# Three small ScalarE copies of a unit's maxima, queued three slots later

## The chip, the cores and the metric

The kernel runs on one core of one Trainium2 chip. The time is the device time of one execution in microseconds (us); "before" is the median of three runs. One further execution was taken with the hardware profiler, and the views of the profile below are of that one.

Engine names: PE is TensorE's matmuls, PEld its weight loads, DVE is VectorE, ACT is ScalarE, POOL is GpSimd, SP is SyncE, which issues most DMAs.

## The reference

One token sequence `x` (2048 x 576) goes through an attention block with 32 heads of 18 columns and through a GELU MLP with 4608 hidden columns; a gate per token mixes the two. All arrays are float32.

```python
qkv = (x @ wqkv)                      # heads: 32, 18 columns each
scores = einsum("bhqd,bhkd->bhqk", q, k) * 18 ** -0.5
a = einsum("bhqk,bhkd->bhqd", softmax(scores), v) ... @ wo
b = gelu(layernorm(x) @ w1 + b1) @ w2 + b2
g = sigmoid((x * gate_w).sum(-1, keepdims=True))
return g * a + (1 - g) * b
```

## The kernel before, in words

Attention runs over 32 **units**; a unit is one pair of heads and one half (1024) of the queries. Each unit has two stages. The **first stage** (`s1_round`, 32 rounds a unit) multiplies queries by keys with the queries as output rows (L204, one matmul for each head of the pair), and VectorE takes the maximum of each 128 x 512 result (L206). When all rounds of a unit are done, `s1_finish` turns the maxima into two extra rows of the query operand: VectorE's maximum over the four key blocks, negated (L215); three ScalarE copies that round it and lay it out (L216 to L218: `nmh`, the rounded value; `nm`, its negative; `nm2`, its place in the layout); VectorE's sum of pairs, which gives the rest that rounding lost (L222); a transposition (L223); and eight small DMAs that write the rows into the query tile (`qa<-mr`, issued on line 114 by a helper).

The **second stage** (`s2`) multiplies keys by queries with those rows included (L280, 56 rows in place of 54), so that the maximum is already subtracted, and ScalarE's exponential (L282) takes the result out of PSUM into a tile `p` or `ring`. `ps_s2` has two PSUM banks, so a score matmul L280 waits for the exponential of the matmul two before it. The product with the values (L309, `pv`) follows for each pair of steps. First-stage rounds of a later unit are woven between the two heads of a second-stage step, so four score matmuls stand together in TensorE's order: L280, L204, L204, L280.

The MLP fills the rest of TensorE: L548 is the first matmul and L680 the second. Its activation runs on VectorE (L572, bias), ScalarE (L573, bias of the other half; L636, squares; L629, tanh) and POOL (L160). ScalarE also rounds weights (L445) in the first quarter.

The order of the work is written out by the program: `run_due` is called after each piece and counts one **slot**; `defer(n, fn)` queues `fn` so that it is issued n slots later. Each engine then runs its own instructions in the order in which they were issued. `looped[0]` is true once the loop over units has begun. The maxima of unit 0 are finished before that. Two of the 32 units find SP busy with loads (`aside`); their eight DMAs are issued by ScalarE, one a slot.

Of the kernel before, what the change touches and what calls it, by code (L numbers as in the profile page):

```python
# [9 lines left out]
F32 = mybir.dt.float32  # L10
F32R = mybir.dt.float32r
AF = mybir.ActivationFunctionType
# [47 lines left out]
def gated_mix_kernel(ctx: ExitStack, tc: tile.TileContext, x, wqkv, wo, w1, b1, w2, b2, gate_w, out):  # L60
    nc = tc.nc
# [50 lines left out]
    def dma_r(queue, dst, src):  # L112

        queue.dma_start(dst.bitcast(F32), src)
# [5 lines left out]
    def defer(n, fn):  # L120
        later.append((slot[0] + n, fn))
# [87 lines left out]
    def s1_finish(u):  # L209

        m4 = M4.pop(u)
        nm = asm.tile([P, 2, 2, 8], F32, name="nm")
        nm2 = asm.tile([P, 2, 2, 8], F32, name="nm2")
        nmh = asm.tile([P, 2, 8], F32R, name="nmh")
        nc.vector.tensor_reduce(nm[:, 0], m4, axis=AX.X, op=ALU.max, negate=True)  # L215
        nc.scalar.activation(nmh, nm[:, 0], AF.Copy)  # L216
        nc.scalar.activation(nm[:, 1], nmh.bitcast(F32), AF.Copy, scale=-1.0)
        nc.scalar.activation(nm2[:, :, 0, :], nmh.bitcast(F32), AF.Copy)  # L218

        def rows():  # L220
            mr = asm.tile([P, 32], F32, name="mr", bufs=1)
            nc.vector.tensor_reduce(nm2[:, :, 1, :], nm.rearrange("p k a b -> p a b k"), axis=AX.X, op=ALU.add)  # L222
            nc.vector.transpose(mr, nm2.rearrange("p a b c -> p (a b c)"))  # L223
            qa = QA[u % 3]
            aside = slot[0] < ybusy[0]

            def store(h, k):
                r = 64 * h + 54
                c = 32 * k + 16 * h
                dst = qa[r:r + 2, :].rearrange("b (t k n) -> b t k n", k=4, n=32)[:, :, k, :]  # L230
                dma_r(nc.scalar if aside else nc.sync, dst, mr[c:c + 16, :])
            for n in range(8):
                if aside:
                    defer(1 + n, lambda n=n: store(*divmod(n, 4)))
                else:
                    store(*divmod(n, 4))
        defer(2 if looped[0] else 8, rows)

    RING = []
    ybusy = [0]  # L240
# [104 lines left out]
    looped = [False]  # L345

    def take_round():
        u, r = rounds.pop()
        head = s1_round(u, r)
        if r == NR - 1:  # L350
            defer(1, lambda: s1_finish(u))
        return head
# [1029 lines left out]
```

## Time and profile before

| | before |
|---|---|
| time, median of 3 runs | 2275.35 us (2274.24 to 2276.49) |
| time of the profiled execution | 2275.04 us |
| its span, first to last instruction | 2273.2 us |
| PE busy | 2243.9 us (99%) |
| PEld busy | 1647.7 us (72%) |
| DVE busy | 1654.6 us (73%) |
| ACT busy | 1442.5 us (63%) |
| POOL busy | 946.5 us (42%) |
| mean granted clock of TensorE | 0.998 |

Busy times of different engines overlap. Matmuls are pipelined and their ends are modelled, so two matmuls that run one after the other count as busy just as two that run side by side. An engine's idle time is listed with what ended it, its releaser.

### The profile page before, as it was taken

Reading aid. Unit: us, or ns where it says so; the run is one execution under the profiler, and the core shown is the slowest. Engines: PE = TensorE matmul, PEld = TensorE weight load, DVE = VectorE, ACT = ScalarE, POOL = GpSimd, SP = SyncE. Lnnn points to the kernel's source line nnn. Section 1 sums busy time; section 2 is a strip of 40 time slices with the busy share of each in tenths; the row PEclk is TensorE's granted clock in tenths of the full one; section 3 lists DMA queues with packets and bytes.
Section 4 is the critical chain, followed back from the end, with each engine's and each line's share of the span. In section 5 each row is a group of like instructions: output and inputs, shape, how many; then the busy total and the mean of one; then the engine's idle time right before and its main releaser. Section 6 shows DMA issues by size and latency. Waiting matters only on the chain.

```text
span 2273.2 us, 51149 instructions
## 1 busy us (share of the span) xinstructions
PE 2243.9 (99%) x20569; PEld 1647.7 (72%) x20569; DVE 1654.6 (73%) x2889; ACT 1442.5 (63%) x2719; POOL 946.5 (42%) x936
## 2 busy tenths in 40 slices
PE   8999999999999999999999999999999999999999
PEld 7878767777667777677776777677767777777668
DVE  5675777777777787777777877787777777777545
ACT  4223777777776666666666666676666666666661
POOL 4002456666663434443444444434444444444420
PEclk9999999999999999999999999999999999999999
DMA  7755634536483524232363324233365233323355
GB/s 241 259 188 182 195 128 153 157 132 183 142 243 135 168 95 124 98 119 98 94 183 143 119 90 142 85 116 116 121 166 157 97 120 113 106 98 115 106 172 196
DMA packets 163219, 323.62 MB, mean 142 GB/s; under 512 B 59646, under 2 KB 86178, under 8 KB 152146
## 3 DMA queue, kind: packets, MB, share of 16 engines
q1 hardware_dynamic: 158982, 313.57, 43.6%
q10 hardware_dynamic: 4000, 6.78, 0.8%
q8 instruction: 162, 2.65, 0.5%
q14 instruction: 75, 0.61, 0.1%
HBM read 229.07 MB, written 95.16 MB: 143 GB/s over the span
## 4 chain that ended last, share of the span: by engine, by line
PE 91%; DVE 4%; DMA 3%; ACT 2%; issue 0%; SPq 0%; POOL 0%; ACTq 0%; DVEq 0%
PE ps L309 20%; PE ps L548 19%; PE ps L680 18%; PE ps L280 13%; PE ps L204 11%; PE ps L956 5%; DVE m L206 2%; PE ps L974 2%; PE ps L1264 1%; PE ps L871 1%; DMA ka<-ot_scr 0%; ACT p L282 0%; DMA dn_scr<-dn 0%; DMA x<-ot_scr 0%; PE ps L1005 0%
## 5 line engine op out<-in xcount | busy, mean ns | idle before, releaser
L206 DVE TENSOR_REDUCE m<-ps 128x1 f32<-128x512 f32 x2048 | 1302.6, 684 | 324.5 <-PE ps L204 293.2
L282 ACT ACTIVATE p<-ps 128x512 f32<-128x512 f32 x1368 | 743.1, 596 | 370.0 <-PE ps L204 275.3
L280 PE MATMUL ps<-qa,ka 56*128 56x512 f32 x2048 | 712.7, 415 | 13.4 <-ACT p L282 6.8
L204 PE MATMUL ps<-ka,qa 54*128 54x512 f32 x2048 | 650.5, 418 | 3.6 <-DVE m L206 2.4
L280 PEld LDWEIGHTS ps<-qa,ka 56*128 56x128 f32 x2048 | 359.8, 185 | 246.3 <-issue 100.1
L680 PE MATMUL ps<-w,hh 64*128 64x288 f32 x4352 | 528.0, 297 | 1.5 <-DVE x L654 0.8
L548 PE MATMUL ps<-big,w 64*128 64x512 f32 x3888 | 517.6, 392 | 0.6 <-POOL w L160 0.5
L160 POOL TENSOR_SCALAR zz<-zz 128x512 f32<-128x512 f32 x272 | 168.8, 621 | 799.6 <-ACT zz L636 793.9
L282 ACT ACTIVATE ring<-ps 128x512 f32<-128x512 f32 x680 | 369.2, 595 | 187.3 <-PE ps L204 135.8
L548 PEld LDWEIGHTS ps<-big,w 64*128 64x128 f32 x3888 | 395.1, 185 | 60.1 <-POOL w L160 0.9
L680 PEld LDWEIGHTS ps<-w,hh 64*128 64x128 f32 x4352 | 418.7, 186 | 15.8 <-PE ps L680 1.3
L160 POOL TENSOR_TENSOR zz<-zz,z 128x512 f32<-128x512 f32 x280 | 361.4, 1291 | 34.9 <-ACT zz L638 10.5
L680 PE MATMUL ps<-w,hl 64*128 64x288 f32 x2176 | 358.4, 292 | 0.0
L204 PEld LDWEIGHTS ps<-ka,qa 54*128 54x128 f32 x2048 | 336.6, 185 | 29.4 <-DVE m L206 9.4
L309 PE MATMUL ps<-p,vt 128*32 128x512 f32 x2736 | 344.5, 598 | 0.0
L680 PEld LDWEIGHTS ps<-w,hl 64*128 64x128 f32 x2176 | 244.0, 186 | 1.2
L160 POOL TENSOR_TENSOR w<-x,w 128x576 fp32r<-128x576 f32 (+1 forms) x34 | 68.3, 2011 | 289.0 <-ACT w L445 286.9
L309 PEld LDWEIGHTS ps<-p,vt 128*32 128x32 f32 x2736 | 71.4, 109 | 152.2 <-issue 146.3
L160 POOL TENSOR_TENSOR hl<-zz,hh 128x512 fp32r<-128x512 f32 x134 | 174.0, 1299 | 15.3 <-ACT hh L599 4.5
L309 PE MATMUL ps<-ring,vt 128*32 128x512 f32 x1360 | 179.1, 598 | 0.0
L654 DVE SCALAR_TENSOR_TENSOR x<-ps,x 128x288 f32<-128x288 f32 x270 | 110.9, 452 | 90.1 <-PE ps L680 87.8
L956 PE MATMUL ps<-big,wqk 128*128 128x512 f32 x504 | 123.6, 400 | 0.0
(119 smaller groups left out, 1380.4 us busy)
## 6 DMA issues: line engine op xcount, KB each, us to landing
w<-w_scr SPq DMA_DIRECT2D x54, 1152.0 KB
w<-w_scr SPq DMA_DIRECT2D x108, 576.0 KB
w_scr<-w SPq DMA_DIRECT2D x18, 1152.0 KB
w_scr<-w SPq DMA_DIRECT2D x36, 576.0 KB
qa<-qk_scr SPq DMA_DIRECT2D x192, 72.0 KB
ka<-qk_scr SPq DMA_DIRECT2D x90, 144.0 KB
x<-in_B_w_dram SPq DMA_DIRECT2D x34, 288.0 KB
qk_scr<-hh SPq DMA_DIRECT2D x36, 256.0 KB
```

The lines of the kernel that those rows point to most:

```text
L160: fn(*args, **kw)
L204: nc.tensor.matmul(ps, qa[r0:r0 + 54, t * P:(t + 1) * P], ka[r0:r0 + 54, kb * TB:(kb + 1) * TB], start=True, stop=True)
L206: nc.vector.tensor_reduce(M4[u][:, h, t, kb:kb + 1], ps, axis=AX.X, op=ALU.max)
L280: nc.tensor.matmul(ps, ka[r0:r0 + 56, kc * P:(kc + 1) * P], qa[r0:r0 + 56, qb * TB:(qb + 1) * TB], start=True, stop=True)
L282: nc.scalar.activation(RING[n % 3][:, qb, h], ps, AF.Exp, scale=SCALE)
L309: nc.tensor.matmul(OB[u][r:r + 32, :], v[:, k, 19 * h:19 * h + 32], RING[c % 3][:, qb, h, :], start=(k == 0), stop=(k == NT - 1))
L548: nc.tensor.matmul(ps[h], wt[w_][r, c, :], Y[s_][r, c, :], start=(k == 0), stop=(k == 26))
L654: nc.vector.scalar_tensor_tensor(dst, ps[nn][:, :ND], 0.5, b2b[:, cs[nn]] if base else dst, op0=ALU.mult, op1=ALU.add)
L680: mm = nc.tensor.matmul(ps[nn][:, :ND], h_[r, tok], w_[p_][r, cs[nn]], start=(k == 0 or bare and k == 3 * G), stop=(k == 6 * G - 1 or bare ...
L871: nc.tensor.transpose(ps[:, t * P:(t + 1) * P], x_view(tb)[:, t, c * P:(c + 1) * P], ident)
L956: nc.tensor.matmul(ps, w_[:, c, ms], big[:, s_, :], start=(k == 0), stop=(k == len(prods) - 1))
L974: nc.tensor.matmul(ps[:, :ND], big[:, s_, tok], w_[:, c, cs], start=(k == 0), stop=False)
```

## The change

The three ScalarE copies go into a function `parts`, issued three slots after L215 (two for unit 0) and not with it; the sum of pairs, the transposition and the DMAs (`rows`) are queued from `parts`, so two slots after the copies (eight before the loop) and not after L215.

```diff
         nc.vector.tensor_reduce(nm[:, 0], m4, axis=AX.X, op=ALU.max, negate=True)
-        nc.scalar.activation(nmh, nm[:, 0], AF.Copy)
-        nc.scalar.activation(nm[:, 1], nmh.bitcast(F32), AF.Copy, scale=-1.0)
-        nc.scalar.activation(nm2[:, :, 0, :], nmh.bitcast(F32), AF.Copy)
+
+        def parts():
+            nc.scalar.activation(nmh, nm[:, 0], AF.Copy)
+            nc.scalar.activation(nm[:, 1], nmh.bitcast(F32), AF.Copy, scale=-1.0)
+            nc.scalar.activation(nm2[:, :, 0, :], nmh.bitcast(F32), AF.Copy)
+            defer(2 if looped[0] else 8, rows)
 
         def rows():
...
-        defer(2 if looped[0] else 8, rows)
+        defer(3 if looped[0] else 2, parts)
```

Lines behind this place are three further down in the changed kernel: L282 is L285 there, L573 is L576, L636 is L639; the copies L216 to L218 become L218 to L220, and L222 and L223 become L225 and L226.

The order of instructions on ScalarE, unit 3 (424 us in the profile), before:

```order
L636 ACTIVATE zz<-z 128x512 x2
L282 ACTIVATE p<-ps 128x512 x4
L629 ACTIVATE zz<-zz 128x512
L216 ACTIVATE nmh<-nm 128x16
L217 ACTIVATE nm<-nmh 128x16
L218 ACTIVATE nm_5211<-nmh 128x2x8
L282 ACTIVATE p<-ps 128x512 x2
L629 ACTIVATE zz<-zz 128x512
L282 ACTIVATE ring_2268<-ps 128x512 x4
```

And the same place now:

```order
L639 ACTIVATE zz<-z 128x512 x2
L285 ACTIVATE p<-ps 128x512 x4
L632 ACTIVATE zz<-zz 128x512
L285 ACTIVATE p<-ps 128x512 x2
L632 ACTIVATE zz<-zz 128x512
L285 ACTIVATE ring_2268<-ps 128x512 x2
L218 ACTIVATE nmh<-nm 128x16
L219 ACTIVATE nm<-nmh 128x16
L220 ACTIVATE nm_5211<-nmh 128x2x8
L285 ACTIVATE ring_2268<-ps 128x512 x2
```

The three copies went behind two pairs of exponentials and a tanh.

ScalarE again, unit 8 (737 us), where a bias and two squares of the MLP follow, before:

```order
L216 ACTIVATE nmh<-nm 128x16
L217 ACTIVATE nm<-nmh 128x16
L218 ACTIVATE nm_9960<-nmh 128x2x8
L573 ACTIVATE z<-ps,b1t 128x512
L282 ACTIVATE p<-ps 128x512 x2
L636 ACTIVATE zz<-z 128x512 x2
L282 ACTIVATE p<-ps 128x512 x2
```

Now:

```order
L576 ACTIVATE z<-ps,b1t 128x512
L285 ACTIVATE p<-ps 128x512 x2
L639 ACTIVATE zz<-z 128x512 x2
L218 ACTIVATE nmh<-nm 128x16
L219 ACTIVATE nm<-nmh 128x16
L220 ACTIVATE nm_9960<-nmh 128x2x8
L285 ACTIVATE p<-ps 128x512 x2
```

The copies moved from ahead of the bias to right behind the squares and right ahead of a pair of exponentials.

VectorE at the end of unit 0, before the loop (239 to 247 us), before:

```order
L215 TENSOR_REDUCE nm<-m_941 128x16
L572 TENSOR_SCALAR ring_2268<-ps,b1t 128x512
L206 TENSOR_REDUCE m_2514<-ps 128x1 x2
L222 TENSOR_REDUCE nm_2456<-nm 128x2x8
L223 STREAM_TRANSPOSE mr<-nm_2456 128x32
L206 TENSOR_REDUCE m_2514<-ps 128x1 x4
```

Now:

```order
L215 TENSOR_REDUCE nm<-m_941 128x16
L575 TENSOR_SCALAR ring_2268<-ps,b1t 128x512
L206 TENSOR_REDUCE m_2514<-ps 128x1 x4
L225 TENSOR_REDUCE nm_2456<-nm 128x2x8
L226 STREAM_TRANSPOSE mr<-nm_2456 128x32
L206 TENSOR_REDUCE m_2514<-ps 128x1 x2
```

The sum of pairs and the transposition went behind one more round's pair of maxima. TensorE's and POOL's orders are the same as before.

## The prediction

> **What bounds the kernel now.** I read the page's busy times first, then the chain that ended last, then TensorE's waits, then the groups of the three instructions that move.
>
> ```profile
> span 2273.2 us, 51149 instructions
> PE 2243.9 (99%) x20569; PEld 1647.7 (72%) x20569; DVE 1654.6 (73%) x2889; ACT 1442.5 (63%) x2719; POOL 946.5 (42%) x936
> ...
> PE 91%; DVE 4%; DMA 3%; ACT 2%; issue 0%; SPq 0%; POOL 0%; ACTq 0%; DVEq 0%
> ```
>
> TensorE (PE) is busy for all but 2273.2 - 2243.9 = 29.3 us, and the chain runs over it for 91%. No other engine is near its limit, so only what TensorE waits for, or what makes its matmuls run less side by side, can be gained. Its waits, in us in total, times, longest:
>
> ```profile
> PE ps L280 <- ACT p L282: 6.8, 9, 0.8
> PE ps L280 <- ACT ring L282: 5.4, 7, 0.8
> ```
>
> These two make 16 waits and 12.2 us, by the second-stage score matmul (L280) for an exponential (L282) that must empty a PSUM bank. Who makes ScalarE late there is told by the first of the three moved instructions:
>
> ```profile
> L216 ACT ACTIVATE nmh<-nm x32: 215/216/218, 239.6 to 2137.9; 128x16 fp32r<-128x16 f32 x32
> ...
>   DVE nm L215: 31.7, 31
> ```
>
> ScalarE sits idle 31.7 us in front of L216, at 31 of its 32 places, until VectorE has made the maximum L215. One such place, in order of time (start, us, engine, line; in brackets the idle time before it and its releaser):
>
> ```profile
> 422.68 0.40 PE L280 MATMUL ps<-qa,ka 56*128 56x512 f32 x1
> 423.77 0.22 DVE L215 TENSOR_REDUCE nm<-m 128x16 f32<-128x64 f32 x1
> 424.03 0.22 ACT L216 ACTIVATE nmh<-nm 128x16 fp32r<-128x16 f32 x1 [1.21 <-DVE nm L215]
> 424.50 1.06 ACT L282 ACTIVATE p<-ps 128x512 f32<-128x512 f32 x2
> 425.13 0.49 PE L280 MATMUL ps<-qa,ka 56*128 56x512 f32 x1 [0.80 <-ACT p L282]
> 426.12 0.64 PE L309 MATMUL ps<-p,vt 128*32 128x512 f32 x4
> ```
>
> The scores of 422.68 were done at 423.08, and ScalarE was idle; but its queue is in order, and L216 stood in front of the exponential, waiting for a maximum that came at 424.00. The exponential began 1.42 us late and TensorE stood for 0.80 us. Such places go from this kind to the last and smallest one:
>
> ```profile
> 1040.81 0.49 PE L280 MATMUL ps<-qa,ka 56*128 56x512 f32 x1 [0.80 <-ACT ring L282]
> 1041.72 0.64 PE L309 MATMUL ps<-p,vt 128*32 128x512 f32 x4
> ...
> 2138.99 0.98 PE L280 MATMUL ps<-qa,ka 56*128 56x512 f32 x2 [0.55 <-ACT ring L282]
> 679.45 0.50 PE L280 MATMUL ps<-qa,ka 56*128 56x512 f32 x1 [0.40 <-ACT p L282]
> ```
>
> I count 14 of 0.80 us and one of 0.55. The sixteenth (679.45) comes 6 us after its L216 and has another cause, DMAs issued by ScalarE; it stays.
>
> **The change part by part.** Nothing is removed or added; three copies per unit go to a later place of ScalarE's queue, and L222, L223 (VectorE) and the eight DMAs (SP's queue, at two units ScalarE's) follow.
>
> *The waits themselves.* Three slots later L215 has long ended, so L216 does not wait and the exponential goes first. The 15 waits vanish: 12.2 - 0.40 = 11.8 us. What is late next at these places: the first exponential would start at about 423.1 instead of 424.50, so TensorE is held by nothing there.
>
> *What the waits do to the matmuls behind them.* After the wait the four score matmuls take 426.12 - 425.13 = 0.99 us until L309 starts, and 1041.72 - 1040.81 = 0.91 at the other. Where nothing waited:
>
> ```profile
> 301.98 0.39 PE L280 MATMUL ps<-qa,ka 56*128 56x512 f32 x1
> ...
> 302.57 0.64 PE L309 MATMUL ps<-p,vt 128*32 128x512 f32 x4
> 737.12 0.39 PE L280 MATMUL ps<-qa,ka 56*128 56x512 f32 x1
> ...
> 737.67 1.07 PE L309 MATMUL ps<-ring,vt 128*32 128x512 f32 x8
> ```
>
> That is 0.59 and 0.55 us. All of it is booked as busy, so the 29.3 us of idle time do not show it. The difference lies between 0.91 - 0.59 = 0.32 and 0.99 - 0.55 = 0.44; I take 0.33, since most of the 14 long waits look like the one at 1040.81, for 15 places: 4.9 us. The lower bound is nothing, the upper 6.6.
>
> *The copies' new place, good kind.* They take 424.50 - 424.03 = 0.47 us of ScalarE wherever they stand. At most places they now fall behind a pair of exponentials, in the idle time in which ScalarE had waited for L215 anyway (0.53 and 1.21 us at the two places shown): no cost, and the cover is that idle time. At six places (the first at 363, the last at 2077) a pair of MLP bias and squares follows, and there the copies now stand behind the squares:
>
> ```profile
> 363.22 0.22 ACT L216 ACTIVATE nmh<-nm 128x16 fp32r<-128x16 f32 x1 [0.53 <-DVE nm L215]
> ...
> 363.70 0.67 ACT L573 ACTIVATE z<-ps,b1t 128x512 f32<-128x512 f32 x1
> 366.26 1.09 ACT L282 ACTIVATE p<-ps 128x512 f32<-128x512 f32 x2
> 366.92 0.49 PE L280 MATMUL ps<-qa,ka 56*128 56x512 f32 x1
> 367.40 0.50 PE L280 MATMUL ps<-qa,ka 56*128 56x512 f32 x1
> ```
>
> The second L280 starts 0.48 after the first because it waits for the second exponential (366.26 + 1.09 = 367.35). Without the copies L573 can start up to 0.48 + 0.53 = 1.01 us earlier, if its input is there; I take 0.6, of which the copies behind the squares give back 0.47. So about 0.13 is gained there, and I put 0.07 on the pair before, whose exponentials come 0.6 earlier: 0.2 times 6 is 1.2 us (bounds: nothing, and 6 times 1.01 - 0.47, 3.2).
>
> *The copies' new place, bad kind.* At four places L573 starts only when its matmuls are done, so it gains nothing when the copies leave:
>
> ```profile
> 737.38 0.69 ACT L573 ACTIVATE z<-ps,b1t 128x512 f32<-128x512 f32 x1 [0.21 <-PE ps L548]
> 740.06 1.09 ACT L282 ACTIVATE p<-ps 128x512 f32<-128x512 f32 x2
> 741.04 0.39 PE L280 MATMUL ps<-qa,ka 56*128 56x512 f32 x1
> 741.28 0.42 PE L280 MATMUL ps<-qa,ka 56*128 56x512 f32 x1
> ```
>
> Here the exponentials move from 740.06 to 740.53; the second ends at 741.62, and the L280 of 741.28 waits for it, 0.34 to 0.39 us. The pair stretches as at 366.92, so I take 0.25 for three places: 0.75 us lost (bounds 0 and 4 times 0.39 = 1.6). The fourth (unit 15) loses a DMA issue from the same spot in exchange and is counted as nothing.
>
> *The start.* Unit 0 is finished before the loop, and its rows are waited for already:
>
> ```profile
> 243.62 0.18 DVE L222 TENSOR_REDUCE nm<-nm 128x16 f32<-128x32 f32 x1
> 243.90 0.21 DVE L223 STREAM_TRANSPOSE mr<-nm 128x32 f32<-128x32 f32 x1
> 244.04 1.29 DVE L206 TENSOR_REDUCE m<-ps 128x1 f32<-128x512 f32 x2
> ...
> 244.14 5.41 SPq L114 DMA_DIRECT2D qa<-mr  x8
> ...
> 250.65 0.79 PE L280 MATMUL ps<-qa,ka 56*128 56x512 f32 x1 [0.66 <-DMA qa<-mr]
> ```
>
> L222 now stands behind the pair of maxima that starts at 244.04 and ends at 245.33. It had followed the pair before it, of the same length, which ended at 243.70. So L223 and SP's eight DMAs start 1.63 us later, and the L280 of 250.65 too: 1.63 us lost, with nothing to hide it. Around it the clock is halved:
>
> ```profile
> 247.25:250.67 3.42, 2.30 (x19) 1.43 (x19) 2.30 (x5) 3.25 (x7) 3.05 (x3) 1.00 0.05 9
> 250.67:257.49 6.82, 6.82 (x41) 5.82 (x43) 4.42 (x7) 5.09 (x10) 3.81 (x3) 0.50 0.59 172
> ```
>
> (Window, length, busy time of PE, PEld, DVE, ACT and POOL, then the granted clock, the DMA share and GB/s.) The halved stretch follows a stretch of 3.42 us with 1.12 us idle; none of the 0.80 us waits brought one. The longer wait adds idle time here. If a further 3.41 us stretch runs at 0.50, another 1.7 us goes; if the wait merely lies inside the halved stretch, 0.8 us comes back. I take nothing for it. [...]
>
> *The rows of the other 31 units.* L222 and L223 move behind two or four more maxima, that is one or two groups of score matmuls further.
>
> ```profile
> 739.79 5.29 SPq L114 DMA_DIRECT2D qa<-mr  x8
> ...
> 751.29 0.39 PE L280 MATMUL ps<-qa,ka 56*128 56x512 f32 x1
> ```
>
> This is one of the tightest units on SP. Its last issue ends at 745.08, its first L280 comes at 751.29, and at the start the landing took 250.65 - 244.14 - 5.41 = 1.10: 5.1 us to spare. Two groups are 741.04 - 737.12 = 3.92 us, so even this unit keeps over 1 us. At some units a weight load that stood right behind the rows on SP now stands ahead of them. At the two units whose DMAs ScalarE issues, they go one pair of exponentials further. POOL's order stays as it is. Cost: nothing; the bound on the other side is rival 4.
>
> *Sum.* -11.8 - 4.9 - 1.2 + 0.75 + 1.63 = -15.5 us. The profiled execution took 2275.04 us (span 2273.2), 0.3 under the median of the three runs, so 2259.5 against 2275.04, or **2259.8 us** against 2275.35 (0.7% less). A measurement of this kernel can tell about 0.2%, 4.6 us, from no change.
>
> **The rivals.**
> 1. *Only the idle time comes back.* The stretch behind the waits belongs to that place and not to the wait. Against it: the two unstalled groups shown belong to other units and are alike. Without the 4.9 us: 2264.7.
> 2. *The halved clock lasts one stretch longer.* 2259.8 + 1.7 = 2261.5.
> 3. *The copies collide at every new place,* as at 741: 0.25 at all 31 instead of three, 7.0 us more: 2266.8. Against it stands a weight copy that takes over twice 0.47 us and stands between exponentials too, while every 0.8 us wait stands 1.1 us behind an L216:
>
> ```profile
> L445 ACT ACTIVATE w<-x 128x1152 fp32r<-128x1152 f32 x16 | 18.6, 1165 | 0.0
> ```
>
> 4. *Slower: the rows come too late.* The first L280 of each unit waits for the DMAs. It takes a shift above the 5.1 us to spare; each us beyond costs 31. At a shift of 5.6 us the 15.5 are gone; at 6.0 it is 2259.8 + 28 = 2288. It would need a third group of maxima ahead of L222, or SP held by a load.
> 5. *Nothing is gained,* because TensorE is held at the same places by a filler's input or a bank of VectorE: 2275. Against it: in the first example TensorE's next work was the four matmuls, and its maxima were done at 423.77.
>
> **How the numbers follow.** The forecast 0.62; rival 1 0.12, rival 2 0.12, rival 3 0.07, rival 4 0.04, rival 5 0.03. The first four cases are faster by more than 0.2% (0.93, of which I leave 0.01 to the unmeasured), no change is 0.04, slower 0.04. The range goes down by the upper bounds of the stretch and of the good places (1.7 + 2.0) to 2256, and up to rival 3, 2267; rivals 1 and 2 lie inside.
>
> **What would show it.** L216's new line has no idle time released by L215; TensorE's waits for L282 fall from 16 to a handful, none over 0.5 us; no four-matmul group before L309 takes 0.9; the wait for the rows at about 250 us grows from 0.66 to about 2 us and no other unit waits for them; new short waits stand only where squares precede the copies. Wrong would be: new waits at L280 for `qa<-mr`, or the 0.8 us waits moved to another pair.

## The result, and the profile after

The changed kernel takes 2261.06 us (median, 2260.56 to 2262.71), the kernel before 2275.32 us beside it (2274.24 to 2276.49, four runs). The ratio is 0.9938, with a 95% interval of 0.9921 to 0.9956. So the change gains 14.3 us; 15.5 were forecast. The profiled execution of the changed kernel took 2260.64 us.

The first lines of the profile's page of the changed kernel, and TensorE's waits in it (total us, times, longest):

```profile
span 2258.9 us, 51149 instructions
PE 2238.7 (99%) x20569; PEld 1643.0 (73%) x20569; DVE 1650.3 (73%) x2889; ACT 1441.9 (64%) x2719; POOL 946.4 (42%) x936
```

```profile
...
PE ps L283 <- DMA qa<-mr: 2.2, 2, 1.5
PE ps L204 <- DVE m L206: 2.2, 4, 0.6
PE ps L683 <- DMA w<-w_scr: 2.1, 1, 2.1
...
PE ps L283 <- ACT p L285: 0.5, 1, 0.5
```

The span is 14.3 us shorter (2273.2 to 2258.9). TensorE's idle time fell from 29.3 to 2258.9 - 2238.7 = 20.2 us, which is 9.1; the other 5.2 us are busy time that went away, on balance (2243.9 to 2238.7): matmuls run side by side again where they had queued behind a wait, as the stretch of four below shows. Of the 16 waits for the exponential (12.2 us) one is left, 0.5 us, and it is the one with another cause. But there is a wait that was not there before: 2.1 us of the second MLP matmul (L683) for a reload of its weights.

The copies no longer wait for VectorE. Of the first of them, L218, the profile says this; nothing stands under "sat idle", and one weight load (0.8 us, not a matmul) is put down to it:

```profile
L218 ACT ACTIVATE nmh<-nm x32: 200/220/237, 240.2 to 2126.5; 128x16 fp32r<-128x16 f32 x32
its engine sat idle before it (us, times) until:
who waited for it (us, times):
  PEld ps L283: 0.8, 1
```

And the place in unit 3 that the prediction showed, now (start, us, engine, line):

```profile
422.79 1.09 ACT L285 ACTIVATE p<-ps 128x512 f32<-128x512 f32 x2 [0.28 <-PE ps L283]
...
425.23 0.23 ACT L218 ACTIVATE nmh<-nm 128x16 fp32r<-128x16 f32 x1
...
423.79 0.40 PE L283 MATMUL ps<-qa,ka 56*128 56x512 f32 x1
...
424.44 1.92 PE L312 MATMUL ps<-p,vt 128*32 128x512 f32 x16
```

The exponential waits for the score matmul only, the copies follow 2.4 us behind it, TensorE stands nowhere, and the four score matmuls take 424.44 - 423.79 = 0.65 us instead of 0.99. At all fifteen places that had waited, the group of four now takes 0.34 to 0.66 us to the product with the values; it took 0.91 to 1.05.

### The profile page after: what moved, and what is told of

Same layout as the page of the kernel before. It is cut to its first block, busy times and chain, and to the rows that moved or that the text cites. A ratio compares the mean times of both kernels' runs of the same rounds, so it can differ in the third digit from the quotient of the medians.

```text
span 2258.9 us, 51149 instructions
## 1 busy us (share of the span) xinstructions
PE 2238.7 (99%) x20569; PEld 1643.0 (73%) x20569; DVE 1650.3 (73%) x2889; ACT 1441.9 (64%) x2719; POOL 946.4 (42%) x936
## 4 chain that ended last, share of the span: by engine, by line
PE 95%; DMA 2%; DVE 2%; ACT 0%; issue 0%; POOL 0%; SPq 0%; ACTq 0%; DVEq 0%
PE ps L312 21%; PE ps L551 20%; PE ps L683 20%; PE ps L283 14%; PE ps L204 11%; PE ps L959 5%; PE ps L977 2%; PE ps L1267 1%; PE ps L874 1%; DMA big<-y_scr 1%; DVE m L206 0%; DMA dn_scr<-dn 0%; DMA w<-w_scr 0%; PE ps L1008 0%; DVE x L1194 0%
## 5 line engine op out<-in xcount | busy, mean ns | idle before, releaser
L285 ACT ACTIVATE p<-ps 128x512 f32<-128x512 f32 x1368 | 743.2, 596 | 380.7 <-PE ps L204 256.0
L683 PE MATMUL ps<-w,hh 64*128 64x288 f32 x4352 | 529.6, 297 | 1.5 <-DVE x L657 0.8
L285 ACT ACTIVATE ring<-ps 128x512 f32<-128x512 f32 x680 | 369.2, 595 | 190.2 <-PE ps L204 122.1
L683 PEld LDWEIGHTS ps<-w,hh 64*128 64x128 f32 x4352 | 420.1, 186 | 16.0 <-DVE x L657 1.0
L683 PE MATMUL ps<-w,hl 64*128 64x288 f32 x2176 | 362.9, 292 | 0.0
L683 PEld LDWEIGHTS ps<-w,hl 64*128 64x128 f32 x2176 | 247.5, 186 | 1.3
```

Of the source, the lines that this page charges most:

```text
L285: nc.scalar.activation(RING[n % 3][:, qb, h], ps, AF.Exp, scale=SCALE)
L683: mm = nc.tensor.matmul(ps[nn][:, :ND], h_[r, tok], w_[p_][r, cs[nn]], start=(k == 0 or bare and k == 3 * G), stop=(k == 6 * G - 1 or bare ...
```

## The experiments

Each was compared with the kernel before on its own chip: the first four on one where that takes 2274.34 us (2273.00 to 2275.82), the other four on a second one, at 2274.15 us (2273.38 to 2275.62). Medians of different sets are compared by what each gains over its own kernel before. "Gain of a unit" below means this: in both traces I take the start of each unit's first second-stage score matmul, subtract, and look at what the difference grows by from unit to unit. The second stage of a unit holds the copies of the next one; a place is named by the unit whose copies stand in it. Unit 23 alone is named by its second stage, in which the reload falls; the stall there belongs to the copies of unit 24.

### 1. The rows later, the copies left where they were

Against the kernel before:

```diff
-        defer(2 if looped[0] else 8, rows)
+        defer(5 if looped[0] else 10, rows)
```

> The three ScalarE copies stay right behind L215 as before; only the sum of pairs, the transposition and the DMAs go three slots later (for unit 0 two), to the places that the change gave them. Theory (the wait in ScalarE's queue is all of it): the 15 waits of 0.8 us stay, TensorE waits 16 times and about 12 us for L282, the time is that of before plus the start's 0.6 to 1.6 us: 2275.3 to 2277. Rival (it is VectorE that gained, because L222 and L223 no longer stand between its additions and maxima): a good part of the 14 us is here, 2262 to 2270.

Measured: 2283.54 us (2280.69 to 2284.34), ratio 1.0038 (1.0025 to 1.0051). It is slower, and by more than either expectation. TensorE's waits:

```profile
PE ps L280 <- ACT p L282: 6.9, 9, 0.8
...
PE ps L280 <- ACT ring L282: 5.4, 7, 0.8
...
PE ps L680 <- DMA w<-w_scr: 2.1, 1, 2.1
```

The 16 waits stay as they were, so they belong to the copies alone; putting VectorE's two instructions off gains nothing. The new wait for the reload comes with the rows alone. In this profile (2280.69 us) the loss is 5.6 us of span: 2.6 at unit 23, where the reload is, 0.14 to 0.23 at eight of the fifteen stalled places, 0.5 at another and 0.7 at unit 15, the other 0.3 at the start and in small amounts. Why later rows cost 0.2 at a stalled unit is open, but it is there in the changed kernel too: those eight places gain 1.10 to 1.21 us in it, five of the others 1.24 to 1.37. The other four executions took 1.9 to 3.7 us longer than the profiled one and have mean clocks of 0.997 or 0.998 against its 0.999; more halved stretches would do that, but no trace of them was taken.

### 2. The copies later, the rows left where they were

Against the changed kernel:

```diff
-            defer(2 if looped[0] else 8, rows)
+            defer(1 if looped[0] else 8, rows)
...
-        defer(3 if looped[0] else 2, parts)
+        if looped[0]:
+            defer(1, parts)
+        else:
+            parts()
```

The order on VectorE and on SP is that of the kernel before; only ScalarE's differs.

> In the loop the copies go one slot later and the rows one slot behind them, so VectorE's and SP's orders are those of before and only ScalarE's differs; unit 0 as before. Theory: all 15 waits go, the start's loss goes too, and if the 2.1 us wait for a weight reload near 1681 us (with 3.4 us of half clock behind it) comes from TensorE being early, it stays: 2260.3; if it comes from the later rows on SP, it goes: 2256.7. Rival (the rows' later place is needed): L222 waits for the copies and VectorE's maxima hold TensorE, over 2265.

Measured: 2256.73 us (2255.11 to 2258.36), ratio 0.9924 (0.9907 to 0.9940). The wait for the reload is gone, as the theory of the late rows says: fourteen of the fifteen stalled places gain 1.18 to 1.39 us each, unit 23 among them (1.29). The median is the 2256.7 of that theory, but by luck, for it hides a new loss that was not expected: unit 7, the fifteenth, loses 1.09 us. On TensorE (the second-stage score matmul is L286 in this kernel, its exponential L288), and on ScalarE:

```profile
672.05 0.79 PE L286 MATMUL ps<-qa,ka 56*128 56x512 f32 x1 [1.75 <-ACT p L288]
```

```profile
667.12 1.06 ACT L288 ACTIVATE p<-ps 128x512 f32<-128x512 f32 x2
669.40 1.95 ACTq L114 DMA_DIRECT2D qa<-mr  x2
671.40 0.60 ACT L288 ACTIVATE p<-ps 128x512 f32<-128x512 f32 x1 [3.22 <-DMA qa<-mr]
```

Unit 7 is one of the two whose rows ScalarE sends. ScalarE was free at 668.18; the first DMA was issued only at 669.40. The semaphore that its issue waits for is raised at 669.33 by the landing of one of SP's loads (`big<-y_scr`; in the kernel before at 676.72, and the DMA is issued at 676.80), and ScalarE's order holds the exponential behind it until 671.40. In the kernel before this was the sixteenth wait, of 0.40 us.

### 3. Unit 0 back at its old place

Against the changed kernel:

```diff
-        defer(3 if looped[0] else 2, parts)
+        if looped[0]:
+            defer(3, parts)
+        else:
+            parts()
```

> The changed kernel with unit 0, before the loop, as it was. The prediction priced the start at 1.63 us: 2259.4. The trace of the changed kernel says that half of that lay inside the halved clock, net 0.6: 2260.5. The wait for the rows at about 250 us goes back from 1.5 to 0.7 us. In neither case does the wait near 1681 us change.

Measured: 2260.77 us (2257.16 to 2261.70), ratio 0.9936 (0.9921 to 0.9951). Over its own kernel before it gains 13.6 us, and the changed kernel gains 14.3 over its own; the intervals overlap almost wholly. So the whole time shows no price of the start, and settles neither the 1.63 us of the prediction nor 0.6. The trace does not settle it either: its profiled execution reaches the second stage of unit 1 by 1.8 us sooner than that of the changed kernel, but the halved clock at the start lasted 3.41 us in it and 6.83 us in the other, which is worth 1.7 us. The wait for the reload stays (2.72 us here).

### 4. The copies on GpSimd, right behind VectorE's maximum, the rows late

Against the kernel before:

```diff
-        nc.scalar.activation(nmh, nm[:, 0], AF.Copy)
...
+        one = dict(op0=ALU.mult, op1=ALU.mult)
+        nc.gpsimd.tensor_scalar(nmh, nm[:, 0], 1.0, 1.0, **one)
...
-        defer(2 if looped[0] else 8, rows)
+        defer(5 if looped[0] else 8, rows)
```

> The copies run on GpSimd right behind L215, rows at the changed kernel's places, unit 0's rows as before: ScalarE is rid of the copies altogether. Theory (what is left of their cost is the ten places where they stand next to bias and squares): L285 waits gone as in the changed kernel, and at those places the second L283 of a pair no longer waits for its exponential, up to 0.25 to 0.5 each: 2.5 to 4 us below the changed kernel with unit 0 back, 2256.5 to 2258. Rival (the new places cost nothing): equal to it, 2260.5. A third: GpSimd's activation chain is held by the wait and TensorE waits for its results, over 2262.

Measured: 2258.20 us (2255.84 to 2260.58), ratio 0.9928 (0.9913 to 0.9942). It tells the places apart. At the three places where the copies now collide with exponentials, the changed kernel loses 0.36, 0.40 and 0.38 us (units 8, 18 and 27); with the copies off ScalarE the losses are -0.04, 0.03 and 0.05. So the collision is what costs there. The reload's wait stays, as it must with late rows.

### 5. Unit 23 alone with early rows

Against the changed kernel:

```diff
-            defer(2 if looped[0] else 8, rows)
+            defer((1 if u == 23 else 2) if looped[0] else 8, rows)
...
-        defer(3 if looped[0] else 2, parts)
+        defer((1 if u == 23 else 3) if looped[0] else 2, parts)
```

> The changed kernel, but for unit 23 alone the copies go one slot behind L215 and the rows one slot later, so its transposition stands where it stood before; SP's order is the same as in the changed kernel. Theory (twelve loads of the next MLP input stand behind unit 23's rows on SP, and the rows' transposition now comes late, so all of SP's queue and at its end the weight reload come late): the 2.1 us wait near 1681 and the half clock behind it go, 3.8 us less than the changed kernel: 2257.2. Rival (TensorE simply arrives earlier at that reload): the wait stays, 2261.

Measured: 2256.99 us (2256.33 to 2257.41), ratio 0.9923 (0.9907 to 0.9940). It gains 17.2 us over its own kernel before, 2.9 more than the changed kernel, and the intervals of the two ratios overlap, so the whole time alone would not show it. The traces do: the changed kernel loses 2.72 us at unit 23, this one gains 1.09 there, so 3.81 us come back, and the wait for the reload is gone. The rival, that TensorE had merely become too early for the reload, would have left the wait: TensorE comes to it at 1679.71 here, and came at 1679.48 in the changed kernel. SyncE's queue in the kernel before, in the changed kernel and in this one, around that unit:

```profile
1649.81 5.24 SPq L114 DMA_DIRECT2D qa<-mr  x8
1655.15 10.51 SPq L114 DMA_DIRECT2D big<-y_scr  x12
...
1680.94 1.83 SPq L114 DMA_DIRECT2D w<-w_scr  x4
```

```profile
1641.22 5.55 SPq L114 DMA_DIRECT2D qa<-mr  x8
1646.87 10.22 SPq L114 DMA_DIRECT2D big<-y_scr  x12
...
1672.54 1.86 SPq L114 DMA_DIRECT2D w<-w_scr  x4
```

```profile
1638.35 5.55 SPq L114 DMA_DIRECT2D qa<-mr  x8
1644.00 10.10 SPq L114 DMA_DIRECT2D big<-y_scr  x12
...
1669.43 1.91 SPq L114 DMA_DIRECT2D w<-w_scr  x4
```

Behind the rows stand twelve large loads of the MLP's input, and behind these the weights' reload. SP issues what is behind the loads as they land, one after the other: in the changed kernel it stands 6.8 us for them before the four stores L332 alone. So the reload follows the first load by nearly the same time in all three, 25.79, 25.67 and 25.43 us, and a delay of the rows reaches it through the loads. The reader of the weights in the kernel before and in the changed one:

```profile
1692.44 0.29 PE L680 MATMUL ps<-w,w 64*128 64x288 f32 x2
```

```profile
1681.58 0.40 PE L683 MATMUL ps<-w,w 64*128 64x288 f32 x2 [2.10 <-DMA w<-w_scr]
```

By the change TensorE was there at 1681.58 - 2.10 = 1679.48, 12.96 us earlier than before; the reload was issued only 1680.94 - 1672.54 = 8.40 us earlier. Of these 4.56 us, 2.10 became a wait, so about 2.5 had been to spare. With the rows early it is issued 11.51 us earlier, and nothing waits.

### 6. Copies later, and ScalarE's own DMAs three slots later

As experiment 2, and against that

```diff
-                    defer(1 + n, lambda n=n: store(*divmod(n, 4)))
+                    defer(4 + n, lambda n=n: store(*divmod(n, 4)))
```

> The kernel in which the copies alone move (one slot), with the DMAs that ScalarE issues at units 7 and 15 three slots later, where the changed kernel has them. Theory (the first of these DMAs waits for a load on SP and holds the exponentials behind it; later, it waits less): the 1.75 us wait at 672 us falls to about 0.45, and with it the 3.4 us of half clock behind it goes: 2256.7 - 1.3 - 1.7 = 2253.7. Rival (the wait follows TensorE's pace, not the DMA's place): 2256.7.

Measured: 2251.92 us (2251.25 to 2252.83), ratio 0.9902 (0.9887 to 0.9916). Better than expected: the wait of unit 7 does not just shrink to what it was, it vanishes, since the first DMA now stands behind a pair of exponentials where its semaphore has just been raised, and the DMAs stand one at a time between exponentials:

```profile
669.12 1.09 ACT L288 ACTIVATE p<-ps 128x512 f32<-128x512 f32 x2 [0.99 <-PE ps L204]
669.74 1.24 ACTq L114 DMA_DIRECT2D qa<-mr  x1
671.03 0.60 ACT L288 ACTIVATE p<-ps 128x512 f32<-128x512 f32 x1 [0.83 <-PE ps L286]
```

Unit 7 goes from a loss of 1.09 us (experiment 2) to a gain of 2.29.

### 7. As 6, but the copies of units 8, 15, 18 and 27 stay right behind the maximum

Against experiment 6:

```diff
-            defer(1 if looped[0] else 8, rows)
+            defer((2 if u in (8, 15, 18, 27) else 1) if looped[0] else 8, rows)
...
-        if looped[0]:
+        if looped[0] and u not in (8, 15, 18, 27):
             defer(1, parts)
```

> The kernel before this one in the call, with the copies of units 8, 15, 18 and 27 alone back right behind L215, ahead of the bias. The traces say that these units lose 0.36 to 0.40 us when the copies stand behind bias or squares: 4 times 0.37 = 1.5 us less than the kernel with the later DMAs: 2252.2. If those losses come from something else that moved: equal to it.

Measured: 2251.09 us (2249.98 to 2252.27), ratio 0.9898 (0.9883 to 0.9913). At units 8, 18 and 27 the loss falls from 0.38, 0.39 and 0.49 us to 0.03, 0.03 and 0.05, 1.15 us together; 1.5 were expected with unit 15. That one gains 0.15 more, but it varies by 0.5 us between kernels that have the same order there (see below), so nothing follows from it. The medians are 0.8 apart, less than their spread, so the whole time alone would not show it.

### 8. GpSimd's copies, early rows, ScalarE's DMAs later

The three copies as in experiment 4, the rows at their slots of the kernel before, ScalarE's DMAs as in 6.

> Copies on GpSimd right behind L215, rows where they were before, ScalarE's DMAs three slots later. If GpSimd's queue is free in time: ScalarE has no copies at all, about 1.5 us less than the kernel with the later DMAs (the three to ten places with bias and squares): 2252.2. Rival: GpSimd is inside a 1.3 us operation when the maxima come, L222 waits on VectorE and TensorE's first-stage matmuls wait for banks: over 2256.

Measured: 2250.21 us (2249.08 to 2251.04), ratio 0.9894 (0.9879 to 0.9908). This is the lowest median: 23.9 us below the kernel before, and the interval lies below that of the changed kernel, 0.9921 to 0.9956. From experiment 7 it cannot be told apart, since the times of the two overlap. Next to nothing is lost at the colliding places (0.01 each), and the six places of the good kind gain 0.54 to 0.71 us instead of 0.34 to 0.45. Against the changed kernel GpSimd is busy for 20 us more and ScalarE for 12 less:

```profile
PE 2231.5 (99%) x20569; PEld 1643.4 (73%) x20569; DVE 1651.9 (73%) x2889; ACT 1429.8 (64%) x2623; POOL 966.8 (43%) x1032
```

## Why the prediction was right, and where its errors cancelled

The forecast of 2259.8 us lies 1.3 below the median, inside the range. Its main mechanism is the one that acts. But one step was wrong by about 4 us, and smaller terms made up for most of it, so that the total comes so close is partly luck. Worked out by gains of units, from the traces of before and after:

| step | forecast, us | measured, us |
|---|---|---|
| waits and the stretch behind them, 15 places | -16.7 | -16.8 at 14 places, and about -1.1 at unit 23 |
| good kind, six places | -1.2 | -2.3 |
| bad kind, three places | +0.75 | +1.1 |
| unit 15 | 0 | +0.5 |
| start | +1.63 | +0.6 |
| rows of the other 31 units | 0 | +3.8 |
| rest, and a start of the run 0.45 earlier | | -0.2 |
| sum | -15.5 | -14.4 |

*The waits, and the stretch behind them.* Right. Experiment 2 moves the copies alone and gets the gain, experiment 1 moves the rest alone and gets none. The 14 places gain 1.10 to 1.37 us each, 1.20 in the mean; the forecast was 0.80 + 0.33. That the gain is larger than the wait of 0.80, and that the four matmuls take 0.65 where they took 0.91 to 0.99, refutes rival 1: the stretch belonged to the wait, and it went at all fifteen places. Rival 5 (nothing gained) falls with it.

*The good kind.* Undersized by half. The value was picked between 0 and 3.2 us, and 2.3 came. Where the copies are off ScalarE (experiment 8) the same six places gain 3.9 us (0.54 to 0.71 each), so the copies behind the squares still take some of it.

*The bad kind, and rival 3.* The mechanism is right, as experiments 4 and 7 show. The size is not 0.25 but 0.36 to 0.40 us, about the upper bound of 0.39. In the changed kernel:

```profile
734.03 0.20 ACT L220 ACTIVATE nm<-nmh 128x16 f32<-128x16 f32 x1
734.13 1.06 ACT L285 ACTIVATE p<-ps 128x512 f32<-128x512 f32 x2
...
734.76 0.50 PE L283 MATMUL ps<-qa,ka 56*128 56x512 f32 x1
735.25 0.50 PE L283 MATMUL ps<-qa,ka 56*128 56x512 f32 x1
```

The copies push the pair of exponentials to 734.13, and the second score matmul waits for the second of them: the two stand 0.49 apart, where they were 0.24 apart in the kernel before (741.04 and 741.28). It stays at these places; at the five other places in the loop no unit lost more than 0.06, so rival 3 did not come. Unit 15, put at nothing, lost 0.52 in this trace, and why is open: it lost 0.70 in experiment 1, where its copies stay in place, and nothing in experiment 3, which has the order of the changed kernel there.

*The start.* The wait came as forecast and cost a third of it in this pair of executions. TensorE's wait there, and the stretch of halved clock around it (length, then busy time of PE, PEld, DVE, ACT and POOL, granted clock, DMA share, GB/s):

```profile
251.79 0.79 PE L283 MATMUL ps<-qa,ka 56*128 56x512 f32 x1 [1.47 <-DMA qa<-mr]
```

```profile
249.49:256.32 6.83, 5.34 (x26) 3.60 (x25) 3.96 (x7) 4.47 (x10) 3.22 (x4) 0.50 0.32 99
```

The matmul is late by 251.79 - (250.65 - 0.45) = 1.59 us, against 1.63 forecast (0.45 us is how much earlier this run was there). But of the halved stretch only 5.34 us are now busy and not 6.82, so about 0.7 us of work ran later at full clock. The prediction named this ("0.8 us comes back") and took nothing for it; it should have been taken.

In this pair the halved stretch lasts 6.83 us in both, so rival 2 (one stretch more) does not show. But it is not refuted. With early rows of unit 0 (the kernel before and experiments 2, 3, 4, 6, 7 and 8) the halved stretch at the start lasts 3.41 us in five of seven profiled executions, and 6.83 in the kernel before and in experiment 8; with late rows (the changed kernel, experiments 1 and 5) it is 6.83 in all three. The five with 3.41 reach the second stage of unit 1 by 1.2 to 1.7 us sooner than the profiled kernel before. So the 0.6 holds between two executions that both had the longer stretch, and whether late rows bring it more often is open.

*The rows of the other units: the step that failed.* The prediction checked whether the rows would reach their own reader in time, found at least 1 us to spare, and wrote "Cost: nothing". That was true of the rows: no unit but the first waits for them, so rival 4 did not come as it was written. It was not true of what is queued behind them. SP's queue is in order, and at unit 23 the late rows held twelve loads and a reload, whose reader had about 2.5 us to spare, 40 us further on. I had seen that weight loads change places with rows, and did not follow one to its reader. And the wait brought a halved stretch with it, in the changed kernel:

```profile
1676.26:1679.68 3.42, 3.22 (x32) 1.47 (x24) 2.81 (x6) 3.27 (x7) 1.58 (x2) 1.00 1.01 399
1679.68:1683.09 3.41, 1.51 (x18) 1.48 (x18) 0.96 (x3) 0.86 (x2) 2.20 (x3) 1.00 1.00 393
1683.09:1686.50 3.41, 3.41 (x28) 3.41 (x28) 1.66 (x3) 2.42 (x5) 0.00 (x0) 0.50 0.15 57
```

The wait is 2.10 us, the halved stretch costs half of 3.41, 1.7 us: 3.8. The changed kernel loses 2.72 us at this unit where it should have gained 1.1, the same 3.8. Experiment 5 gives 3.81 us back by the rows of that one unit. The DMA share of 1.01 and 1.00 in the first two rows (399 and 393 GB/s) shows the DMA engines busy throughout while TensorE waits.

*What would show it.* Held: no idle time before the first copy, no wait for the exponential above 0.5 us, no long group of four at the moved places, longer waits for the rows at the start (two, 2.2 us together) and at no other unit. Not held: that new waits stand only where squares precede the copies; the largest new wait is for a DMA that the list did not name.

The halved stretches in these traces are 3.41 or 6.83 us long. The one at 1683.09 follows a stretch in which TensorE was busy for 1.51 us of 3.41.

## What to carry to other kernels

An instruction that waits in an in-order queue costs what stands behind it, and the gain of taking it out of the way is the wait plus the slower matmuls after it (here 0.80 and about 0.40 us). When a step is put off, follow each queue that its instructions stand in to the end, its DMAs too: the price is paid by whoever reads the load behind them (here 3.8 us at a matmul that comes 40 us after the rows). Move only the instructions that block (the three copies) and leave the rest of the chain early, as experiments 2, 6, 7 and 8 do.

## What the runs showed of the hardware

- A DMA issued by ScalarE can hold ScalarE. In experiment 2 the first of eight was issued only 1.22 us after ScalarE was free, when a load of SP's had landed, and two issues took 1.95 us; the exponentials behind them waited 3.22 us. Issued later, one by one (experiment 6), each stood for 0.62 to 1.24 us between exponentials and cost TensorE nothing.
- A wait of TensorE does not always bring a halved stretch. The 1.75 us wait of experiment 2, the 2.10 us wait of the changed kernel and the 2.22 us wait of experiment 4 did; the 2.14 us wait of experiment 1 and the 2.72 us wait of experiment 3 did not, in their profiled executions. The last of them lay across two stretches of 3.41 us, the length of that run's halved stretch at the start, counted on from it:

```profile
1675.15:1678.56 3.41, 2.11 (x20) 1.24 (x16) 1.57 (x4) 1.91 (x4) 2.77 (x4) 1.00 1.02 397
1678.56:1681.97 3.41, 1.94 (x22) 1.90 (x24) 1.26 (x3) 1.30 (x3) 1.00 (x1) 1.00 0.89 341
```

  Yet 2.30 us busy of 3.42 was enough for the fall in the kernel before. So the busy time of a stretch alone does not tell when the clock falls, and what does is open. The other executions of experiment 3 took 3.0 to 4.5 us longer than the profiled one at a lower mean clock (0.997 or 0.998 against 0.999), which fits a halved stretch that comes in some executions and not in others.
- GpSimd's copy of 128x16 takes as long as ScalarE's:

```profile
L218 POOL TENSOR_SCALAR nm<-nmh x32: 204/205/207, 241.3 to 2114.6; 128x16 f32<-128x16 f32 x32
```

  The median is 205 ns, against 200 to 220 ns for the same copies on ScalarE.
